# Loading the caches and large weights from GpSimd's DMA queue, one packet per engine and transfer

## The chip, the cores and the metric

The kernel runs on one core of a Trainium2 chip. Its engines are TensorE (PE, whose weight loads the profile shows as PEld), VectorE (DVE), ScalarE (ACT), GpSimd (POOL) and SyncE (SP), and sixteen DMA engines move data between the chip's main memory (HBM) and the on-chip memory (SBUF). The metric is the device time of one execution in microseconds; lower is better. Before the change three runs gave 2522.07, 2522.24 and 2522.47 us, a median of 2522.24.

## The reference, cut to what matters

One decode step of an attention block with a cache of 65,536 positions and 32 heads, and beside it a small gated feed-forward block; a sigmoid gate mixes the two. All inputs are bfloat16.

```python
q = (x @ wq).reshape(1, 1, 32, 128).transpose(0, 2, 1, 3)         # x: 1x1x512, wq: 512x4096
scores = einsum("bhqd,bhkd->bhqk", q, k_cache) * 128 ** -0.5      # k_cache: 1x32x65536x128
p = softmax(scores, axis=-1)
o = einsum("bhqk,bhkd->bhqd", p, v_cache)                         # v_cache: 1x32x65536x128
a = o.transpose(0, 2, 1, 3).reshape(1, 1, 4096) @ wo              # wo: 4096x512
b = (silu(x @ w_gate) * (x @ w_up)) @ w_down                      # 512x1792, 512x1792, 1792x512
g = sigmoid((x * gate_w).sum(-1, keepdims=True))
out = g * a + (1 - g) * b
```

The two caches are 512 MiB each. Every byte of them is used once, so the kernel reads 1,088 MB and computes little on each byte.

## The kernel before, in words

Each head's cache of 65,536 positions is laid over the 128 partitions, 512 positions to a partition, so that a partition's share is one contiguous run of 128 KB. A head is cut into three pieces of 168, 168 and 176 positions per partition (`CUTS`), which makes 96 pieces of K and 96 of V. A piece of 168 is 128 runs of 43,008 bytes, 5.5 MB; a piece of 176 is 128 runs of 45,056 bytes.

SBUF holds a ring of four slots (`SLOTS`), each as large as the largest piece. `big` takes the slot that has been free longest; `load` (L139 to L148) takes a slot and issues the transfer of one piece at L147, in one transfer or, for a few pieces, in several. The query weights `wq` and the feed-forward weights pass through the same ring at the start, and the output weights at the end.

The main loop runs over the K pieces n = 0 to 95. At stage n it issues the load of K piece n and then that of a V piece v that lies up to five pieces behind. It then computes:

- `products` (L304, L308), on DVE: K times the query, in place, and then three halving additions, which leave 16 columns for each position.
- `scores` (L325), on PE: matmuls with the identity add these columns up three at a time into PSUM; this is the last use of the K piece and frees its slot. `add_up` (L343) on DVE finishes the sum one stage later.
- at a head's end `row_max` and `exponentials`: maximum over the head, then the exponentials on ACT.
- `values` (L401), on PE: one matmul for each four positions, against the V piece; the last one frees V's slot.

A load is issued as soon as the last reader of its slot's old content is done. That reader is PE, in `scores` for a slot that held K and in `values` for one that held V. All issues but one stand in SyncE's queue, in program order, and each waits at its head of the queue for its slot and for its completion counter to be free. The one other, `x_row`, is issued by ACT.

SyncE also issues 40 small loads of output-weight rows (`load_tall`, L208) at five places of the main loop, which the matmuls of `project_tall` use nine stages later. After the loop the last V pieces are loaded in up to five transfers each, and `load_wo` (L237) issues the rest of the output weights in ten transfers: five of 512 KB, three of 256 KB and two of 128 KB. The end is the projection (L513), a copy on ACT and the store of the result (L637).

GpSimd does nothing but set constants and build the identity (`make_identity`, behind L97) in the first 1.3 us. The order of all instructions on each engine is the program's (`manual_schedule`).

Of the kernel before, what the change touches and what calls it, by code (L numbers as in the profile page):

```python
# [35 lines left out]
def kernel(  # L36
# [14 lines left out]
    nc = tc.nc  # L51
# [6 lines left out]
    KT = D // P  # L58
    FT = F // P
# [25 lines left out]
    def big(name):  # L85
        slot = free.pop(0)
        t = ring.tile([P, SLOT * Dh], bf16, name=name, tag=f"big{slot}")
        return t, slot
# [4 lines left out]
    gw_row = small.tile([1, D], bf16, name="o_row")  # L93
    wq_t, wq_slot = big("wq_t")
    wq_sb = wq_t[:, : KT * H * Dh].rearrange("p (t f) -> p t f", t=KT)
    nc.sync.dma_start(out=wq_sb, in_=A_wq.rearrange("(p t) f -> p t f", t=KT))
    nc.scalar.dma_start(out=x_row, in_=A_x[0])  # L97

    ident_f = consts.tile([P, P], f32, name="ident_f")
# [36 lines left out]
    def span(n):  # L136
        return CUTS[n % G], CUTS[n % G + 1]

    def load(dst, cache, n, name, cuts=None):  # L139
        h = n // G  # L140
        a, b = span(n)
        t, taken[name, n] = big(name)
        view = t[:, : (b - a) * Dh].rearrange("p (j d) -> p j d", d=Dh)
        src = cache[0, h, :, :].rearrange("(p j) d -> p j d", p=P)
        cuts = cuts or (0, b - a)
        for c, d in zip(cuts[:-1], cuts[1:]):
            nc.sync.dma_start(out=view[:, c:d, :], in_=src[:, a + c : a + d, :])  # L147
        dst[n] = view  # L148

    load(K_tiles, A_k_cache, 0, "K_t", (0, span(0)[1] // 2, span(0)[1]))  # L150
    load(K_tiles, A_k_cache, 1, "K_t")

    def queries(g):
# [17 lines left out]

    gu_t, gu_slot = big("gu_t")
    wgu_sb = gu_t[:, : 2 * KT * F].rearrange("p (w t f) -> p w t f", w=2, t=KT)
    nc.sync.dma_start(out=wgu_sb[:, 0], in_=B_w_gate.rearrange("(p t) f -> p t f", t=KT))
    nc.sync.dma_start(out=wgu_sb[:, 1], in_=B_w_up.rearrange("(p t) f -> p t f", t=KT))
    wd_sb = gu_t[:, 2 * KT * F : 2 * KT * F + FT * D].rearrange("p (t n) -> p t n", t=FT)
    nc.sync.dma_start(out=wd_sb, in_=B_w_down.rearrange("(p t) n -> p t n", t=FT))
    nc.sync.dma_start(out=gw_row, in_=gate_w.rearrange("(o d) -> o d", o=1))
    WG = 4
    wo_tiles = {}  # L180
# [46 lines left out]
    def load_wo():  # L227
        t = big("wo_t")[0]
        for g in range(1, H // WG):
            at = (g - 1) * WG * D  # L230
            wo_tiles[g] = t[:, at : at + WG * D].rearrange("p (t n) -> p t n", t=WG)
            rows = A_wo[g * WG * P : (g + 1) * WG * P, :]
            last = g == H // WG - 1
            rows = rows.rearrange("(t p) n -> p t n" if last else "(p t) n -> p t n", t=WG)
            cuts = (0, 2, 3, 4) if last else (0, 2, 4) if g == H // WG - 2 else (0, 4)
            for a, b in zip(cuts[:-1], cuts[1:]):
                nc.sync.dma_start(out=wo_tiles[g][:, a:b, :], in_=rows[:, a:b, :])  # L237

    def feed_forward_in():

# [298 lines left out]
    rows = {}  # L539
# [15 lines left out]
    for n, v in steps:  # L555
        if n > 1:
            load(K_tiles, A_k_cache, n, "K_t")
# [64 lines left out]
    head_column(H - 2, O_parts)  # L622
    load(V_tiles, A_v_cache, N - 1, "V_t", V_CUTS[N - 1])
    load_wo()
    values(N - 3, 88)
    values(N - 2)
# [41 lines left out]
```

## Time and profile before

| what | value |
|---|---|
| median of three runs | 2522.24 us (2522.07 to 2522.47) |
| span of the profiled execution, first to last instruction | 2520.4 us (the profile gives no other time of it) |
| DMA traffic | 1,088.41 MB in 31,101 packets, 432 GB/s over the span |
| SyncE's DMA queue (q1) | 31,046 packets, 99.9% of sixteen engines' span |
| DVE busy | 2234.4 us, 89% |
| PE busy | 1408.6 us, 56% |
| ACT busy | 103.4 us, 4% |
| GpSimd (POOL) busy | 0.7 us |
| PE waiting for V loads, in total | 774.9 us |
| DVE waiting for K loads, in total | 163.1 us |

The profile is of one execution. Its page gives busy times for each engine, the span in 40 slices with the DMA engines' busy share and rate, the packets of each DMA queue, and the chain of work that ended last, followed back from the last instruction. Besides the page the trace can be asked for windows of time, for the chain in order of time, for what each engine waited for, and for single instructions. It holds a record of every DMA packet with its queue, start, length and bytes. An engine's name with a small q (SPq) is its queue of DMA issues.

### The profile page before, as it was taken

How to read it: one execution, taken by the hardware profiler on the slowest of the kernel's cores; microseconds unless marked ns; L12 is line 12 of the kernel's file. 1: busy time of each engine (PE TensorE's matmuls, PEld its weight loads, DVE VectorE, ACT ScalarE, POOL GpSimd, SP SyncE). 2: the span in 40 equal slices, each digit the busy share in tenths (PEclk: the TensorE clock that was granted, in tenths of full speed). 3: DMA queues.
4: the chain of work that ended last, by engine and by line, in shares of the span. 5: the costliest groups of instructions: out<-in, count | busy, mean ns of one | idle time of the engine just before them, and what ended most of it. 6: DMA issues, size and time to landing. Idle time of an engine off the chain costs nothing.

```text
span 2520.4 us, 12122 instructions
## 1 busy us (share of the span) xinstructions
PE 1408.6 (56%) x5174; PEld 488.2 (19%) x5174; DVE 2234.4 (89%) x788; ACT 103.4 (4%) x314; POOL 0.7 (0%) x6
## 2 busy tenths in 40 slices
PE   2555546565555654655546565554564655556468
PEld 1111112121121211211212121111121211112123
DVE  7999998988989889999889998889999889898880
ACT  1000000000000000000000000000000000000000
POOL 0000000000000000000000000000000000000000
PEclk7677767676776766677767777776677777777779
DMA  9999999999999999999999999999999999999999
GB/s 420 430 439 433 433 431 435 431 433 434 434 432 436 433 434 433 432 434 433 431 434 435 435 433 431 434 433 433 433 433 433 436 434 434 433 432 431 434 434 390
DMA packets 31101, 1088.41 MB, mean 432 GB/s; under 512 B 3532, under 2 KB 4048, under 8 KB 5192
## 3 DMA queue, kind: packets, MB, share of 16 engines
q1 hardware_dynamic: 31046, 1087.65, 99.9%
q8 instruction: 40, 0.66, 0.1%
q14 instruction: 13, 0.11, 0.0%
q10 hardware_dynamic: 2, 0.00, 0.0%
HBM read 1087.64 MB, written 0.00 MB: 432 GB/s over the span
## 4 chain that ended last, share of the span: by engine, by line
DMA 59%; DVE 23%; PE 17%; issue 1%; ACT 0%; SPq 0%; DVEq 0%
DMA V_t<-in_A_v_cache_dram 45%; DMA K_t<-in_A_k_cache_dram 14%; PE O_ps L401 13%; DVE K_t L304 11%; DVE K_t L308 10%; PE part_ps L325 3%; DVE S_sb L343 0%; PE mT_ps L363 0%; DVE m L358 0%; DMA wo_t<-in_A_wo_dram 0%; ACT diag L360 0%; DVE top L370 0%; DVE rg L391 0%; PE a_ps L291 0%; DVE recip L390 0%
## 5 line engine op out<-in xcount | busy, mean ns | idle before, releaser
L401 PE MATMUL O_ps<-V_t,P_sb 128*4 128x512 bf16 x4096 | 1087.3, 434 | 777.8 <-DMA V_t<-in_A_v_cache_dram 774.9
L304 DVE TENSOR_TENSOR K_t<-K_t,q_bc 128x22528 bf16<-128x22528 bf16 (+4 forms) x128 | 1111.9, 8686 | 163.5 <-DMA K_t<-in_A_k_cache_dram 163.1
L308 DVE TENSOR_TENSOR K_t<-K_t 128x5376 bf16<-128x5376 bf16 (+11 forms) x384 | 1016.3, 2647 | 12.2
L401 PEld LDWEIGHTS <-P_sb 128*4 128x4 bf16 x4096 | 383.5, 94 | 1492.8 <-issue 1082.7
L325 PE MATMUL part_ps<-K_t,ident_b 128*128 128x504 bf16 (+2 forms) x640 | 228.8, 506 | 167.9 <-DVE K_t L308 167.9
L325 PEld LDWEIGHTS <-ident_b 128*128 128x128 bf16 x640 | 62.5, 109 | 310.8 <-issue 211.5
L363 PE MATMUL mT_ps<-diag,ones_f 128*128 128x129 f32 (+1 forms) x64 | 24.9, 491 | 130.3 <-ACT diag L360 130.3
L432 ACT ACTIVATE O_sb<-O_ps,ident_f 4x128 f32<-4x128 f32 x120 | 33.2, 346 | 1002.9 <-PE O_ps L401 1002.9
L343 DVE TENSOR_REDUCE S_sb<-part_ps 128x168 f32<-128x504 f32 (+1 forms) x96 | 59.8, 623 | 3.2 <-PE part_ps L325 3.2
L370 DVE TENSOR_REDUCE top<-mT_ps 128x1 f32<-128x128 f32 x32 | 9.3, 292 | 44.8 <-PE mT_ps L363 44.8
L363 PEld LDWEIGHTS mT_ps<-diag,ones_f 128*128 128x128 f32 x64 | 15.6, 303 | 154.6 <-ACT diag L360 154.2
L461 ACT ACTIVATE o_row<-r_sb,rg 1x128 bf16<-1x128 f32 x26 | 10.4, 401 | 581.3 <-DVE r_sb L444 581.3
L439 PE MATMUL r_ps<-O_sb,ones_f 4*1 4x512 f32 x60 | 33.0, 630 | 0.0
L360 ACT ACTIVATE diag<-ident_f,m 128x128 f32<-128x128 f32 x32 | 12.8, 401 | 428.1 <-DVE m L358 428.1
L374 ACT ACTIVATE P_sb<-S_sb,bias 128x512 bf16<-128x512 f32 x32 | 23.1, 722 | 1.0
L358 DVE TENSOR_REDUCE m<-S_sb 128x1 f32<-128x512 f32 x32 | 22.0, 686 | 1.1
L444 DVE TENSOR_REDUCE r_sb<-r_ps 1x128 f32<-1x512 f32 x30 | 20.1, 670 | 0.0
L156 PE MATMUL qg_ps<-wq_t,X_bc 128*128 128x512 bf16 x32 | 9.2, 460 | 10.7 <-DMA wq_t<-in_A_wq_dram 10.7
L390 DVE RECIPROCAL recip<-tot_ps 128x1 f32<-128x1 f32 x1 | 0.2, 168 | 16.6 <-PE tot_ps L385 16.6
L291 PE MATMUL a_ps<-O_sb,ones_f 1*1 1x512 f32 x2 | 1.9, 1030 | 19.7 <-ACT O_sb L290 19.7
L372 ACT ACTIVATE bias<-top 128x1 f32<-128x1 f32 x32 | 6.5, 203 | 41.2 <-DVE top L370 41.2
L246 PEld LDWEIGHTS <-gu_t 128*128 128x128 bf16 x112 | 6.9, 157 | 0.6 <-issue 0.6
(68 smaller groups left out, 88.5 us busy)
## 6 DMA issues: line engine op xcount, KB each, us to landing
K_t<-in_A_k_cache_dram SPq DMA_DIRECT2D x63, 5376.0 KB
V_t<-in_A_v_cache_dram SPq DMA_DIRECT2D x62, 5376.0 KB
K_t<-in_A_k_cache_dram SPq DMA_DIRECT2D x32, 5632.0 KB
V_t<-in_A_v_cache_dram SPq DMA_DIRECT2D x31, 5632.0 KB
V_t<-in_A_v_cache_dram SPq DMA_DIRECT2D x2, 2816.0 KB
K_t<-in_A_k_cache_dram SPq DMA_DIRECT2D x2, 2688.0 KB
V_t<-in_A_v_cache_dram SPq DMA_DIRECT2D x2, 2560.0 KB
wq_t<-in_A_wq_dram SPq DMA_DIRECT2D x1, 4096.0 KB
```

Of the source, the lines that this page charges most:

```text
L304: yield nc.vector.tensor_tensor(out=K, in0=K, in1=q_rep, op=ALU.mult)
L308: yield nc.vector.tensor_tensor(out=K[:, :, 0:half], in0=K[:, :, 0:half], in1=K[:, :, half : 2 * half], op=ALU.add,)
L325: nc.tensor.matmul(part[:, :, 0:take], lhsT=ident_b, rhs=K_tiles[n][:, :, c : c + take], start=(i == 0), stop=(i == len(takes) - 1),)
L343: nc.vector.tensor_reduce(out=S_tiles[h][:, a:b], in_=S_parts.pop(n), axis=AXIS.X, op=ALU.add)
L358: nc.vector.tensor_reduce(out=m, in_=S_tiles[h], axis=AXIS.X, op=ALU.max)
L360: nc.scalar.activation(out=diag[:, :P], in_=ident_f, func=ACT.Copy, scale=m)
L363: nc.tensor.matmul(mT_ps[:, :wide], lhsT=ones_f, rhs=diag[:, :wide], start=True, stop=True)
L374: nc.scalar.activation(out=P_tiles[h], in_=S_tiles[h], func=ACT.Exp, bias=bias, scale=scale, accum_out=new_sum(h),)
L401: nc.tensor.matmul(O_tiles[h], lhsT=P_tiles[h][:, a + j : a + j + 4], rhs=V_tiles[n][:, j : j + 4, :], start=(a + j == 0), stop=(a + j == ...
L432: nc.scalar.activation(out=O_sb[:, c * Dh : (c + 1) * Dh], in_=O_ps[:, c * Dh : (c + 1) * Dh], func=ACT.Copy, scale=ident_f[0:4, c : c + 1],)
L439: nc.tensor.matmul(r_ps, lhsT=ones_f[0:4, 0:1], rhs=O_sb, start=True, stop=True)
L444: nc.vector.tensor_reduce(out=r_sb, in_=r_ps.rearrange("o (c d) -> o d c", c=4), axis=AXIS.X, op=ALU.add)
```

## The change

[...] For a K or V piece an engine's part is eight runs, one for each of eight partitions. Sizes, order and destinations stay. `x_row` stays on ACT; `gate_w`, the 40 small output-weight loads and the store of the result stay on SyncE.

```diff
-    nc.sync.dma_start(out=wq_sb, in_=A_wq.rearrange("(p t) f -> p t f", t=KT))
+    nc.gpsimd.dma_start(single_packet=True, out=wq_sb, in_=A_wq.rearrange("(p t) f -> p t f", t=KT))
...
         for c, d in zip(cuts[:-1], cuts[1:]):
-            nc.sync.dma_start(out=view[:, c:d, :], in_=src[:, a + c : a + d, :])
+            nc.gpsimd.dma_start(
+                out=view[:, c:d, :], in_=src[:, a + c : a + d, :], single_packet=True
+            )
...
-    nc.sync.dma_start(out=wgu_sb[:, 0], in_=B_w_gate.rearrange("(p t) f -> p t f", t=KT))
-    nc.sync.dma_start(out=wgu_sb[:, 1], in_=B_w_up.rearrange("(p t) f -> p t f", t=KT))
+    nc.gpsimd.dma_start(single_packet=True, out=wgu_sb[:, 0], in_=B_w_gate.rearrange("(p t) f -> p t f", t=KT))
+    nc.gpsimd.dma_start(single_packet=True, out=wgu_sb[:, 1], in_=B_w_up.rearrange("(p t) f -> p t f", t=KT))
...
-    nc.sync.dma_start(out=wd_sb, in_=B_w_down.rearrange("(p t) n -> p t n", t=FT))
+    nc.gpsimd.dma_start(single_packet=True, out=wd_sb, in_=B_w_down.rearrange("(p t) n -> p t n", t=FT))
...
-                nc.sync.dma_start(out=wo_tiles[g][:, a:b, :], in_=rows[:, a:b, :])
+                nc.gpsimd.dma_start(
+                    out=wo_tiles[g][:, a:b, :], in_=rows[:, a:b, :], single_packet=True
+                )
```

## The prediction

> **What bounds the kernel.** I read the page from the top: busy times, the 40 slices, the DMA queues, the chain that ended last, the costly groups.
>
> ```profile
> span 2520.4 us, 12122 instructions
> ...
> PE 1408.6 (56%) x5174; PEld 488.2 (19%) x5174; DVE 2234.4 (89%) x788; ACT 103.4 (4%) x314; POOL 0.7 (0%) x6
> ...
> DMA  9999999999999999999999999999999999999999
> GB/s 420 430 439 433 433 431 435 431 433 434 434 432 436 433 434 433 432 434 433 431 434 435 435 433 431 434 433 433 433 433 433 436 434 434 433 432 431 434 434 390
> DMA packets 31101, 1088.41 MB, mean 432 GB/s; under 512 B 3532, under 2 KB 4048, under 8 KB 5192
> ...
> q1 hardware_dynamic: 31046, 1087.65, 99.9%
> q8 instruction: 40, 0.66, 0.1%
> ...
> DMA V_t<-in_A_v_cache_dram 45%; DMA K_t<-in_A_k_cache_dram 14%; PE O_ps L401 13%; DVE K_t L304 11%; DVE K_t L308 10%; PE part_ps L325 3%; DVE S_sb L343 0%; PE mT_ps L363 0%; DVE m L358 0%; DMA wo_t<-in_A_wo_dram 0%; ACT diag L360 0%; DVE top L370 0%; DVE rg L391 0%; PE a_ps L291 0%; DVE recip L390 0%
> ...
> L304 DVE TENSOR_TENSOR K_t<-K_t,q_bc 128x22528 bf16<-128x22528 bf16 (+4 forms) x128 | 1111.9, 8686 | 163.5 <-DMA K_t<-in_A_k_cache_dram 163.1
> L308 DVE TENSOR_TENSOR K_t<-K_t 128x5376 bf16<-128x5376 bf16 (+11 forms) x384 | 1016.3, 2647 | 12.2
> ```
>
> The sixteen DMA engines are busy in every slice, at 430 to 436 GB/s nearly everywhere; queue q1, which is SyncE's, has 99.9% of it. DVE at 89% is the next bound, some 286 us away. PE and DVE wait, in the chain, for K and V loads. So the end is set by how long the DMA engines take over 1,088 MB, plus a start before their first packet and a tail behind their last.
>
> Two things about that DMA time decide this case: what a packet costs besides its bytes, and how early a load is issued. For the first, the windows view (second column of numbers from the right is the DMA share, the last is GB/s):
>
> ```profile
> 2016.00:2457.00 441.00, 243.91 (x872) 82.77 (x872) 396.36 (x133) 16.30 (x51) 0.00 (x0) 0.73 1.00 433
> 2490.00:2500.00 10.00, 9.56 (x45) 3.68 (x44) 0.00 (x0) 0.00 (x0) 0.00 (x0) 1.00 1.00 423
> 2500.00:2505.00 5.00, 4.26 (x20) 1.61 (x19) 0.00 (x0) 0.00 (x0) 0.00 (x0) 1.00 1.00 424
> 2505.00:2510.00 5.00, 5.00 (x24) 1.94 (x23) 0.00 (x0) 0.00 (x0) 0.00 (x0) 1.00 0.97 394
> ```
>
> At a full DMA share the rate is 433 GB/s where the packets are 43,008 and 45,056 bytes, but 423 where the last V pieces and the output weights move 5 to 20 KB at a time: small packets are dearer per byte. The trace's packet records give the size of it: 43,008 bytes take 1.589 us (median of 16,000), 4,096 bytes 0.159 us (median of 648), the 4 bytes of a completion 0.009 us. The slope is 38,912 B / 1.430 us = 27.2 B/ns for one engine, and what is left over is 1.589 - 43,008 / 27,200 = 0.008 us, at 4,096 bytes also 0.008. Each packet costs 8 ns beside its bytes, whatever its size.
>
> For the second, the chain between two heads (start, length, what):
>
> ```profile
> 235.30 36.07 DMA V_t<-in_A_v_cache_dram
> 271.37 0.04 issue
> 271.41 11.93 PE O_ps L401 x42
> 283.34 0.02 issue
> 283.36 27.32 DMA K_t<-in_A_k_cache_dram
> ```
>
> A V load lands 36 us after SyncE issued it, a K load 27.3 us after. Its own 5.5 MB take 12.7 us at 433 GB/s, so a K load stood behind 27.3 - 12.7 = 14.6 us of other transfers, less about 2 us of start and receipt (from the output's issue at 2518.46 us to the end of the span at 2520.4 is 1.9): a lead of some 12.6 us. V has some 21 us. The smallest lead, at the start, is about 5 us (V issued at 94.96, landed 19.8 us later). In steady state a K issue may come 12 us late and the engines still don't run dry.
>
> **The change part by part.**
>
> *Packets.* The moved loads are 97 K and 102 V issues, one wq, three feed-forward weights and ten output weights: 213. They hold 199 x 128 (caches) + 128 (wq) + 384 (feed-forward) + 1,408 (output weights: 5 x 128, 2 x 128, 4 x 128 rows) = 27,392 data packets, 1,712 per engine, and 213 completions per engine. With all of one engine's rows of a load in one packet, up to 1,712 of its 1,925 gaps can go: 1,712 x 8.2 ns = 14.0 us, all on the path, since the DMA engines are never idle. That is the best end. The middle end is nothing, if the 8 ns belong to each contiguous run and not to the packet; the worst end is a loss, if a packet of 344 KB (8 x 43,008) starts less smoothly than one of 43 KB (third rival). The trace can't separate run and packet, since here each run is a packet. The nearest row is the 4-byte completion: 9 ns for a packet with almost no bytes, so the gap goes with the packet's opening and closing. I take most of it, 10 us, and leave 4 us for what each run inside a packet may still cost.
>
> [...]
>
> *The issue moves from SyncE to GpSimd.* SyncE's issue instruction lasts 0.33 us (median of 199 at the load's line). GpSimd has 0.7 us of work in the whole span, all before 1.3 us, so 213 issues find a free queue; what one costs there the trace does not show. Two loads fall due per 25.5 us; between 0.33 us and 5 us an issue lies within the lead of 12.6 us and costs nothing. If that cover were gone, each us past it would cost 97 us, one for each K.
>
> *Start.* wq's issue on SyncE begins at 0.74 us, its first packet some 1.0 us later. GpSimd is past the opening barrier at 0.73, too, so the shift is only the difference in issue latency: between 0 and 3 us (nine times SyncE's issue). I take 0.6, nearer to the rows of SyncE and ScalarE (0.41 and 0.51 us for their first issues). It delays the DMA stream, so it counts in full. The identity that GpSimd builds behind wq's issue is needed at 41.9 us, by the first scores: hidden.
>
> *Tail.* The ten output-weight loads go one by one between 2482.6 and 2511.2 us, held back by earlier landings; the last lands at 2516.95. With a slower issue the DMA share of that stretch, 0.83 to 0.97 already, can lose 0 to 1.5 us. I take 0.5.
>
> *What leaves SyncE's queue.* The 40 small output-weight loads stay on SyncE and no longer stand before a K load (at 211.74 four of them took 9.74 us, waits included). That only lengthens a lead: nothing. An engine that changes queues only between packets would now keep such a load waiting up to 12.7 us in place of 1.6; they are used nine stages (230 us) later: nothing. The instruction fetches (q8, 40 packets of 16 KB; by their number PE's, which has 10,348 of the 12,122 instructions) could wait as long. PE waits 775 us in all for V loads, so a stall of 11 us mostly falls into that; at most 40 x 11 us, taken into the range's upper part.
>
> *Sum.* 2520.4 - 10 + 0.6 + 0.5 = 2511.5 us of span. The three timed runs have a median of 2522.24, 1.8 us above the profiled span (the profiled execution is known by its span alone), so 2513.3: I say 2513. Its own range, with 14.0 or 6 us saved and the small terms at their ends, is 2508 to 2518.
>
> **The rivals.**
>
> *The gap belongs to each run, nothing is saved.* For it: each partition's row is a contiguous run of its own before and after. Against it: the 9 ns of a 4-byte packet. Only start and tail are left: 2523.3, range 2518 to 2528, which is no change.
>
> *DVE holds up GpSimd's issues, and the engines run dry (slower).* Place: K's issue, which always comes just ahead of DVE's longest instruction:
>
> ```profile
> 283.36 0.33 SPq L147 DMA_DIRECT2D K_t<-in_A_k_cache_dram  x1
> ...
> 284.65 11.89 DVE L304 TENSOR_TENSOR K_t<-K_t,q_bc 128x22528 bf16<-128x22528 bf16 x1 [3.11 <-DMA K_t<-in_A_k_cache_dram]
> ```
>
> The K load is issued 1.3 us before L304 starts 11.9 us of work. If GpSimd could not write its descriptors until that instruction ends, the issue would be 13.2 us late, plus 1 us of its own: 14.2 against a lead of 12.6. It decides from there: 1.6 us x 97 = 155 us, 2677. If it needed the next instruction's end also (L308, 5.4 us), 7 us x 97 = 680 us, 3200. If only some issues were caught, 2540 to 2600. For it: DVE is busy 89% of the span. Against it: what these two engines share cannot be seen here, as GpSimd does nothing after 1.3 us.
>
> [...]
>
> *A long packet starts cold (slower).* The first sixteen packets of the run, 32,768 bytes on idle engines, took 1.8 to 2.2 us against 1.21 later: filling the pipe costs 0.6 to 1.0 us. If every load's packet paid that, 213 x 0.75 = 160 us: 2682; a tenth of it gives 2539. For it: nothing shows how descriptors reach the engines from GpSimd. Against it: a load is issued 12 us ahead, which is time to fetch them.
>
> **How the numbers follow.** Three runs of before lie within 0.4 us, so 0.2%, 5 us, is about what can be told from no change. Saved packets 0.50; nothing saved 0.19; issues held up 0.16; cold packets 0.15. The first gives faster, the second the same, the other two slower: 0.50, 0.19, 0.31. The first two fill 2507 to 2528 with 0.69; of the slower 0.31 about 0.11 are mild forms up to 2570, so 2507 to 2570 holds 0.80.
>
> **What would show it.** Right: q1 nearly empty, a queue of GpSimd with 1,087 MB, 434 to 435 GB/s in the steady slices, a DMA share of 1.00, and 43,008 bytes at 1.581 to 1.585 us in the packet records. Nothing saved: 1.589 again and 433 GB/s. Held up: slices with DMA below 9, POOL's queue waiting or its issues lasting as long as L304. Cold: long first packets of each load, and the rate down evenly. The prediction is wrong if the steady rate is below 432 GB/s, or if the landing of a K load is more than 30 us behind its slot's release.

## The result and the profile after

The changed kernel takes 2525.74 us (median of 20 runs, 2525.19 to 2527.21), the kernel before 2522.32 (20 runs, 2522.07 to 2522.49): a ratio of 1.0014, with a 95% interval of 1.0008 to 1.002. It is slower by 3.4 us, 0.14%, clear of the noise and within the 0.2% that the prediction calls no change. The forecast was 2513 us.

The page of the changed kernel (columns as on the page of before; in section 6 the last column is the median time from issue to landing):

```profile
span 2524.4 us, 12148 instructions
...
PE 1412.3 (56%) x5174; PEld 488.7 (19%) x5174; DVE 2234.4 (89%) x788; ACT 103.5 (4%) x314; POOL 113.6 (4%) x219
...
DMA  9999999999999999999999999999999999999998
GB/s 415 432 430 433 434 433 436 432 433 433 433 433 435 432 433 434 436 433 432 432 434 433 435 435 430 433 435 433 434 433 434 431 434 433 433 436 431 433 432 370
DMA packets 30589, 1088.41 MB, mean 431 GB/s; under 512 B 3532, under 2 KB 3536, under 8 KB 4680
...
q0 software_dynamic: 30288, 1087.12, 99.7%
q8 instruction: 40, 0.66, 0.1%
q1 hardware_dynamic: 246, 0.53, 0.1%
...
L147 POOL DMA_DIRECT2D K_t<-in_A_k_cache_dram x97 | 51.3, 529 | 1918.5 <-PE O_ps L405 1523.2
...
K_t<-in_A_k_cache_dram POOLq DMA_DIRECT2D x63, 5376.0 KB, 27.1
V_t<-in_A_v_cache_dram POOLq DMA_DIRECT2D x62, 5376.0 KB, 36.8
```

The traffic has moved to GpSimd's queue (q0), all else is as it was: 430 to 436 GB/s in the steady slices, the DMA engines at 9 tenths or more in all slices but the last. There are 512 packets fewer, not 27,000. An issue costs GpSimd 0.53 us where SyncE needed 0.33, and a K load still lands 27 us after it. In the windows view (last columns granted clock, DMA share, GB/s) the stages that hold 95% of the time have the rates of before to 1 GB/s. The first line is of before, whose second stage the prediction shows, the other two are of after:

```profile
63.00:2016.00 1953.00, 1088.99 (x3856) 368.87 (x3855) 1790.14 (x625) 76.70 (x240) 0.00 (x0) 0.73 1.00 433
...
63.00:2016.00 1953.00, 1089.22 (x3848) 368.54 (x3848) 1790.53 (x626) 76.61 (x239) 79.79 (x151) 0.72 1.00 433
2016.00:2457.00 441.00, 245.06 (x875) 82.88 (x874) 397.53 (x133) 16.50 (x52) 18.11 (x35) 0.74 1.00 434
```

The packet records say the same: 43,008 bytes take 1.589 us (median of 16,000), as before. With each packet's bytes spread evenly over its record, 1,000 MB of the loads have moved 2310.53 us after the first packet, before 2310.47. So in this execution the way between the two ends costs and gains nothing. The profiled execution (2526.15 us itself, its span 2524.4) differs from before's at the ends:

| stretch of the profiled span | before | after | difference |
|---|---|---|---|
| start of the span to the first data packet | 1.77 | 2.62 | +0.85 |
| first data packet to the last | 2515.53 | 2516.20 | +0.67 |
| last data packet to the store's issue | 1.16 | 1.22 | +0.05 |
| store's issue to the end | 1.96 | 4.33 | +2.37 |

The store's issue, before and after:

```profile
2518.46 0.28 SPq L637 DMA_DIRECT2D out_dram<-out_sb  x1
...
2520.04 0.26 SPq L641 DMA_DIRECT2D out_dram<-out_sb  x1
```

The last row of the table is the largest. Beside the kernel's work, the program ends with a meeting: its closing line has drains and semaphore instructions of all five engines. In the changed kernel GpSimd comes to it last, when the other four have drained by 2521.6 us. Its drains, in the source view of the program's closing line (shortest, median and longest in ns, then first and last start), of before and of after:

```profile
L663 POOLq DRAIN  x3: 34/77/386, 1.0 to 2520.2; - x3
```

```profile
L667 POOLq DRAIN  x3: 45/102/10457, 2513.1 to 2524.1; - x3
```

The long one starts at 2513.1 us, with GpSimd's last load issued, and lasts 10.46 us, to 2523.6. That is 4.8 us after the last data packet (2518.82) and 2.0 after SyncE was ready. SyncE's waits in the closing (the sum, how often, the longest; the view names the last engine by its semaphore, not GpSimd) show what it costs, before and after:

```profile
SPq L663 <- PEq L663: 0.6, 2, 0.4
```

```profile
SPq L667 <- PEq L667: 2.7, 2, 2.2
```

### The profile page after: what moved, and what is told of

The parts are those of the page before. It is cut to its first block, busy times and chain, and to the rows that moved or that the text cites. A ratio compares the mean times of both kernels' runs of the same rounds, so it can differ in the third digit from the quotient of the medians.

```text
span 2524.4 us, 12148 instructions
## 1 busy us (share of the span) xinstructions
PE 1412.3 (56%) x5174; PEld 488.7 (19%) x5174; DVE 2234.4 (89%) x788; ACT 103.5 (4%) x314; POOL 113.6 (4%) x219
## 4 chain that ended last, share of the span: by engine, by line
DMA 66%; DVE 18%; PE 13%; issue 3%; ACT 0%; POOL 0%; DVEq 0%; POOLq 0%
DMA V_t<-in_A_v_cache_dram 60%; PE O_ps L405 10%; DVE K_t L308 9%; DVE K_t L312 8%; DMA K_t<-in_A_k_cache_dram 4%; PE part_ps L329 2%; DMA wo_t<-in_A_wo_dram 1%; DMA wq_t<-in_A_wq_dram 1%; DVE S_sb L347 0%; PE qg_ps L158 0%; PE mT_ps L367 0%; DVE m L362 0%; PE a_ps L517 0%; ACT diag L364 0%; PE a_ps L295 0%
## 5 line engine op out<-in xcount | busy, mean ns | idle before, releaser
L147 POOL DMA_DIRECT2D K_t<-in_A_k_cache_dram x97 | 51.3, 529 | 1918.5 <-PE O_ps L405 1523.2
L147 POOL DMA_DIRECT2D V_t<-in_A_v_cache_dram x102 | 53.9, 528 | 451.4 <-PE part_ps L329 344.1
## 6 DMA issues: line engine op xcount, KB each, us to landing
K_t<-in_A_k_cache_dram POOLq DMA_DIRECT2D x63, 5376.0 KB, 27.1
```

The source lines that it names most:

```text
L147: nc.gpsimd.dma_start(out=view[:, c:d, :], in_=src[:, a + c : a + d, :], single_packet=True)
```

## The experiments

Beside each experiment the kernel before was timed on the same chip; its medians are 2522.28 to 2522.39 us. Differences to the changed kernel go by its 2525.74. Line numbers of the experiments differ by a few.

**The option off, and the option on SyncE's queue.** Two changes were made at once, a queue and an option (`single_packet=True`); these take them apart.

```diff
-nc.gpsimd.dma_start(..., single_packet=True)
+nc.gpsimd.dma_start(...)                        # e1_no_option
...
-nc.gpsimd.dma_start(..., single_packet=True)
+nc.sync.dma_start(..., single_packet=True)      # e2_option_on_sp
```

> The changed kernel with the one-packet option taken off every load; the queue stays GpSimd's. Theory (an 8 ns gap belongs to each long run of bytes, the option saves nothing on runs of 43 KB, and the loss lies at the start, in the tail and in the closing): as the changed kernel, 2525.7 us within 0.5, with 43,008 bytes at 1.589 us again. Rival A (the option saves some of the gap and the queue loses more elsewhere): slower than the changed kernel, up to 2539. Rival B (the long packets are what costs): nearer to the kernel before, 2522.3 to 2524.

> The changed kernel with every load issued by SyncE again, the one-packet option left on. Theory: the kernel before, 2522.3 us, packets and all, as the option would have nothing to act on there. Rival A (the option works on either queue): 2508 to 2517.

Measured: 2525.55 us without the option (11 runs, 2525.30 to 2527.08), 2522.37 with it on SyncE's queue (10 runs, 2522.18 to 2522.54), against 2522.38 for the kernel before. The theory held in both. The queue line of the first is the changed kernel's, packet for packet:

```profile
q0 software_dynamic: 30288, 1087.12, 99.7%
```

So the option does nothing here on either queue, and the whole 3.4 us belong to the queue. One packet for all that an engine moves of a transfer, as the title has it, is found in no run; whether the option reached the queues at all, the traces do not tell. The joining of the last output weights' 1 and 2 KB rows, which is where the 512 packets went, is done by GpSimd's queue without it.

**What a run costs.** The cache rows are cut into four runs, on each queue, and then into runs of 2 KB.

```diff
-    nc.sync.dma_start(out=view[:, c:d, :], in_=src[...])
+    nc.sync.dma_start(out=view[:, c:d, :], in_=src[...], max_dma_last_dim=11264)    # e3; 2048 in e5
...
-    nc.gpsimd.dma_start(..., single_packet=True)
+    nc.gpsimd.dma_start(..., single_packet=True, max_dma_last_dim=11264)            # e4; 2048 in e6
```

> The kernel before, with each partition's run of a cache piece cut into four (10,752 or 11,264 bytes). 4,512 runs more per engine for the 188 full pieces and 48 for the cut ones, 4,560 x 8.2 ns = 37.4 us. Every theory: 2559.7 us. It gives the price of a run on SyncE's queue.

> [...] Theory (the gap belongs to the run): 2525.7 + 37.4 = 2563.1 us, packet records of 10,752 bytes at 0.40 us. Rival A (the gap belongs to the packet, and the option makes one packet of all): 2525.7 us.

Measured: 2543.74 us on SyncE's queue, 2544.89 on GpSimd's (four runs each). Both expectations of size missed: on SyncE's queue 4,560 more runs cost 21.4 us, 4.7 ns each, where the packet records leave 8 ns over. On GpSimd's they cost 2544.89 - 2525.74 = 19.2 us, 4.2 ns each, so what one packet would have saved (all of it) is not saved. And the two queues are now 1.15 us apart, not 3.4, of which more below.

> The kernel before with cache rows cut into runs of 2,048 bytes: 31,180 runs more for each engine. By 4.7 ns a run (21.4 us / 4,560 in the quarter cut): 2669 us. By the packet records' 8.2 ns: 2778 us. This is the price for the next.

> The changed kernel with the same runs of 2,048 bytes (168 and more for one engine and transfer). Theory (GpSimd's queue joins runs into packets of 4,096 bytes and no more, as it did with the 1 and 2 KB rows of the last output weights): packet records of 4,096 bytes at 0.159 us and half the added price, 2595 to 2605 us. Rival (nothing is joined): 2,048-byte records and 2657 to 2672 us. Rival (all in one packet): 2526 us.

Measured: 2669.36 and 2612.82 us (two runs each). The first confirms the price. By the pages there are 500,224 packets more than before, 31,264 for each engine where the expectation had 31,180, so a run costs 147.0 us / 31,264 = 4.70 ns. The pages, first on SyncE's queue, then on GpSimd's:

```profile
GB/s 400 409 409 409 409 409 409 409 409 409 409 409 409 409 409 407 409 409 409 408 409 409 410 409 409 409 409 409 409 409 409 409 409 409 409 409 409 409 409 378
DMA packets 531325, 1088.41 MB, mean 408 GB/s; under 512 B 3532, under 2 KB 10448, under 8 KB 530760
...
q1 hardware_dynamic: 531270, 1087.65, 104.6%
```

```profile
GB/s 400 418 418 418 418 418 418 418 418 418 418 418 418 418 418 418 418 418 418 418 419 418 418 418 418 419 418 418 418 418 418 418 418 418 418 418 418 418 418 379
DMA packets 266877, 1088.41 MB, mean 417 GB/s; under 512 B 3532, under 2 KB 3568, under 8 KB 266312
...
q0 software_dynamic: 266576, 1087.12, 101.8%
...
L147 POOL DMA_DIRECT2D K_t<-in_A_k_cache_dram x97 | 133.8, 1380 | 1952.4 <-PE O_ps L406 1574.4
```

GpSimd's queue joins two runs into a packet of 4,096 bytes (260,544 records of that size, none of 2,048): 267 thousand packets in place of 531. The pieces with shorter runs show where it stops: three runs of 1,408, 1,536 or 1,792 bytes make packets of 4,224, 4,608 and 5,376 bytes, four of 1,280 make 5,120. So it joins runs until a packet holds 4,096 bytes or more; the 4,096 bytes "and no more" of the expectation are the case of 2 KB runs.

That costs 87.1 us more than the changed kernel, somewhat over the 70 to 80 expected. Per engine there are 14,768 packets more than in the changed kernel; at 4.70 ns they come to 69.4 us, and the other 17.7 us, over 16,496 joined runs, are 1.1 ns each. If the closing is taken out, which is 2.0 us shorter here than in the changed kernel, they are 1.2 ns. A packet saved is therefore worth 3.5 to 3.6 ns, less than half of the 8 ns that the forecast took from the records. This takes the 4.7 ns of SyncE's queue for GpSimd's too; with the same 2.0 us of closing taken out, the quartered runs cost 4.6 ns there. Runs of 4 KB and more were joined in no run here, with the option or without.

The queue's share on the page of the first, 104.6% of sixteen engines, also says why the records mislead: the records of one engine overlap. A record's length holds time in which the engine already works on the next.

**The ends, by moving loads.** Four kernels give single loads at the ends back to SyncE or, in the last, one load to GpSimd. The lines are shortened; in the first three GpSimd's loads keep the option.

```diff
-    nc.gpsimd.dma_start(single_packet=True, out=wq_sb, ...)                  # e7, and e9
+    nc.sync.dma_start(out=wq_sb, ...)
...
-                nc.gpsimd.dma_start(out=wo_tiles[g][:, a:b, :], ...)         # e8, and e9
+                (nc.gpsimd if g < H // WG - 2 else nc.sync).dma_start(out=wo_tiles[g][:, a:b, :], ...)
...
-                nc.sync.dma_start(out=wo_tiles[g][:, a:b, :], ...)           # e11, from the kernel before
+                (nc.gpsimd if last and b == 4 else nc.sync).dma_start(out=wo_tiles[g][:, a:b, :], ...)
```

> The changed kernel with wq alone issued by SyncE again. The first packet should come 0.85 us earlier (1.77 us as in the kernel before, not 2.62). Theory (start, tail and closing add up, about 0.85 + 0.67 + 2.4 of the profiled span): 2525.7 - 0.85 = 2524.9 us. Rival (the first packet's delay is made up later, since GpSimd's other issues follow it anyway): 2525.7 us.

> The changed kernel with the last five output-weight loads (1 MB) issued by SyncE again; GpSimd's last issue then is some 10 us earlier. Theory (GpSimd's drain ends about 10 us after its last issue begins, and the closing waits for it): the drain ends before the store, the closing falls from 4.3 us after the store's issue to about 2.3, and the tail gets back part of its 0.67: 2523.1 to 2523.8 us. Rival (the closing takes 2 us more whenever GpSimd has issued loads, early or late): 2525.0 to 2525.7.

> Both: wq and the last five output-weight loads by SyncE, the caches and all else by GpSimd. Theory: the two gains add, 2522.3 to 2523.0 us, so the caches alone cost or gain nothing on GpSimd's queue. Rival (the queue costs something in steady state, too): over 2523.5.

> The kernel before, with only the very last output-weight load (128 KB) issued by GpSimd, every other load by SyncE. Theory (drain after GpSimd's last issue): the closing takes 2 us longer with this one load, 2524.3 to 2524.8 us, with a drain of about 10 us in GpSimd's queue. Rival (the closing grows with the 213 loads): 2522.3 to 2522.8.

Measured: 2525.27 (2524.52 to 2526.40), 2525.73, 2525.74 and 2522.72 us, eleven runs each. Only the first is near its theory: 0.47 us less than the changed kernel where 0.85 was expected, in runs that spread over 1.9 us. The other three tested less than I meant, for the same reason. With two queues the order of the program no longer set the order of landing here. SyncE has nothing else to wait for, so it issues the five late loads of the second kernel at 2480.7 us, ahead of output weights that GpSimd issues up to 2504.7. They push back V's last pieces, and from the last packet to the store there are 3.5 us of work left in place of 1.2. The closing did fall in the second kernel, from 4.33 to 2.02 us after the store's issue, but the store came 1.9 us later. The time of the last kernel lies in its rival's range, but there GpSimd issued its only load at 2479.7, not last, so its drain (7.1 us, to 2486.8) was over long before the end, and the 0.4 us say nothing on the closing. The order is lost at the start, too. In the first kernel SyncE issues wq at 0.74 us as before, but GpSimd's first K loads share the engines with it, and the query matmuls start at 17.8 us (in the changed kernel at 14.1):

```profile
0.74 0.41 SPq L96 DMA_DIRECT2D wq_t<-in_A_wq_dram  x1
...
17.83 8.97 PE L158 MATMUL qg_ps<-wq_t,X_bc 128*128 128x512 bf16 x32 [15.52 <-DMA wq_t<-in_A_wq_dram]
```

**The ends, with the last V piece as well.** This was to keep the tail's order by giving SyncE all of it.

```diff
-            nc.gpsimd.dma_start(out=view[:, c:d, :], ..., single_packet=True)
+            if name == "K_t" or n < N - 1: nc.gpsimd.dma_start(..., single_packet=True)
+            else: nc.sync.dma_start(...)        # and wq and all of load_wo on nc.sync
```

> wq, the last V piece and all output weights by SyncE, in the order and with the holding back of the kernel before; all other loads by GpSimd with the option. Theory (all of the loss lies at the two ends): first packet at 1.77 us, GpSimd's drain over before the store, 2522.3 to 2522.8 us. Rival (GpSimd's queue costs something on the way): 2523.5 or more.

Measured: 2534.93 us (five runs), 12.5 over before. The theory's figure failed, and the rival's holds for a reason that is not the rival's. The chain at its end (start, length, what):

```profile
2460.53 48.61 DMA V_t<-in_A_v_cache_dram
2509.13 0.04 issue
2509.18 15.49 PE O_ps L406 x64
2524.67 0.87 PE a_ps L518 x8
2525.55 0.98 PE oc_ps L426 x8
2526.52 5.35 PE a_ps L518 x48
```

The last DMA packet ends at 2519.6 us, 2.3 later than in before, after an equal start. But the V piece that GpSimd issued at 2460.5 took 48.6 us to land, as SyncE's later loads (issued from 2469.4 us) shared the engines with it, and when it was there all of the last matmuls were still to be done. The DMA engines finished almost as early, in the wrong order.

**The closing.** How long after the last landing of GpSimd's loads its drain ends: 0.41 us with 1 load (e11), 4.76 with 213 (the changed kernel), 2.11 with 213 loads of four times the runs (e4), 1.22 with those of 2 KB (e6). That is why the two queues are 1.15 us apart with quartered runs: there the drain is over before the store is, and the closing takes 2.31 us. The author's theory for it, which no trace shows, was that the drain works through finished loads that GpSimd still keeps on lists, and that lists filled by longer loads are cleared sooner. Two experiments: fewer loads, and `dynamic_dma_scratch_size=4096`, which was meant to make the lists smaller.

```diff
-            nc.gpsimd.dma_start(out=view[:, c:d, :], ..., single_packet=True)         # e12
+            if n >= 66: nc.gpsimd.dma_start(..., single_packet=True)
+            else: nc.sync.dma_start(...)        # wq and feed-forward weights on nc.sync
...
-    nc = _bacc.Bacc("TRN2", target_bir_lowering=False, num_devices=1)                 # e14, e15
+    nc = _bacc.Bacc("TRN2", target_bir_lowering=False, num_devices=1, dynamic_dma_scratch_size=4096)
```

> wq, the feed-forward weights and the caches' first two thirds by SyncE; from piece 66 on, and for the output weights, GpSimd: 76 loads in place of 213. GpSimd's closing drain ended 4.76 us after its last landing with 213 loads, 4.71 with 212, 4.49 with 208, 4.45 with 207: 0.052 us per load, and 2.11 with 213 loads of four times as many runs. Theory D (the drain retires the loads that GpSimd has not yet retired, about 85 of 213, and none is retired earlier while there are few): 76 loads cost about 4.3 us after the last landing, the closing is as long as in the changed kernel, 2524.4 to 2525.3 us. Rival (the drain grows with all loads in the run, 4.76 / 213 = 0.022 us each): 1.7 us, which the store covers, 2522.5 to 2523.2 us.

> [...] The quarter-run kernels differed by 1.15 us between the two queues, not 3.4, and there the drain ended 2.11 us after the last landing, not 4.76. Theory (the closing drain works through the finished loads still on the lists; here at most some 28 of them, by 41 ns each 1.5 us, which the store covers): closing 2.3 us after the store's issue, not 4.3, and 2523.4 to 2524.0 us. Rival (the drain depends on the number of loads alone): 2525.3 to 2526 us.

> The same with wq issued by SyncE. Theory (start and closing are all of the loss): first packet at 1.77 us, 0.85 us less than the small ring alone, 2522.6 to 2523.1 us. Rival (the queue costs something on the way): 2523.5 or more.

Measured: 2524.92, 2523.59 and 2523.42 us. With 76 loads the drain ended 3.47 us after the last landing, between the theory's 4.3 and its rival's 1.7, but the closing is only 3.05 us, and the total is mixed with a loss of 2.1 us at the change of queues (the stream falls that far behind the kernel before's between 730 and 760 MB moved), so its falling into the theory's range proves little. It does exclude that every load of the run adds the same: 76 loads cost 73% of what 213 did.

With the scratch size set, the drain costs less: same loads, same order, same queue, and 2.15 us less. What the drain works through is not shown, and no run shows the 28 loads or the 41 ns for each that the expectation adds up; its range held. GpSimd's drain and SyncE's wait:

```profile
L669 POOLq DRAIN  x3: 40/102/7074, 2512.8 to 2521.8; - x3
```

```profile
SPq L669 <- PEq L669: 0.7, 2, 0.5
```

The drain ends 1.36 us after the last landing, inside the time that the store takes anyway, and the closing is 2.33 us. With wq on SyncE besides, the first packet came at 1.76 us as expected, but only 0.17 us were gained; the expectation missed.

## Why the prediction was wrong, point by point

- *Packets*, the step that failed. The forecast took 10 us for packets that would vanish. No run shows that, nor the 6 us saved at the small end of its range. None of the cache's packets vanished: the option changed no packet in any run here, and GpSimd's queue joined only runs under 4 KB. The rival "the gap belongs to each run, nothing is saved", with 2523.3 us and a range of 2518 to 2528, was the right case, with a chance of 0.19; its 2523.3 lacked the closing. The signs that the prediction named for being wrong did not appear (433 GB/s, over its 432; K loads landing in 27.1 us, under its 30). The sign that told was the 1.589 us of a record, for nothing saved.
- *The size of the gap* was wrong as well. A packet's 8 ns in the records is no time lost, since records overlap (104.6% of the engines' span in e5); a run cost 4.7 ns when the number of runs was changed. All 1,712 gaps could have given 8.0 us, not 14.0, and at 3.5 to 3.6 ns for a joined packet 6.0 to 6.2.
- *The nearest row*, the 9 ns of a 4-byte completion, was no argument. Such a completion is a packet and a run, and could not tell one from the other, as the prediction itself had said of the rest.
- *The issue* at no cost was right. It takes 0.53 us in place of 0.33, under a lead of 12.6; K loads land in 27.1 us, before 27.3 for the one shown. At 2 KB runs it takes 1.38 us, and the slices stay level at 418 GB/s.
- *DVE holds up GpSimd's issues* did not happen. The stretch that the prediction showed, in the timeline of after:

```profile
283.51 0.53 POOL L147 DMA_DIRECT2D K_t<-in_A_k_cache_dram  x1 [20.90 <-PE O_ps L405]
...
285.58 11.89 DVE L308 TENSOR_TENSOR K_t<-K_t,q_bc 128x22528 bf16<-128x22528 bf16 x1 [3.19 <-DMA K_t<-in_A_k_cache_dram]
...
285.60 0.53 POOL L147 DMA_DIRECT2D V_t<-in_A_v_cache_dram  x1 [1.56 <-PE part_ps L329]
```

  A V load is issued 0.02 us after DVE starts its longest instruction, and takes 0.53 us. All 199 issues of the caches took 0.528 to 0.552 us (source view of L147), with DVE busy for 89% of the span. The rival's chance of 0.16 was the author's estimate.
- *A long packet starts cold* was not tested: there is no long packet.
- *Start*: 0.6 forecast, 0.85 measured in the profile. GpSimd starts its first issue at 1.25 us, not at 0.73 where its first work behind the opening barrier had started before, and needs 0.67 us for it. Two lines of before, then after:

```profile
0.73 0.20 POOL masks.py:197 MEMSET ident_f<- 128x128 f32 x1 [0.29 <-POOLq L652]
0.74 0.41 SPq L96 DMA_DIRECT2D wq_t<-in_A_wq_dram  x1
...
1.25 0.67 POOL L96 DMA_DIRECT2D wq_t<-in_A_wq_dram  x1 [0.80 <-POOLq L656]
1.91 0.22 POOL masks.py:197 MEMSET ident_f<- 128x128 f32 x1
2.21 0.29 POOL masks.py:199 TENSOR_SCALAR_AFFINE_SELECT ident_f<-ident_f 128x128 f32<-128x128 f32 x1
2.45 1.60 POOL L147 DMA_DIRECT2D K_t<-in_A_k_cache_dram  x3
```

- *Tail*: 0.5 forecast; 0.67 in this profile, but 0.05 in the one without the option and 0.38 in e14, so it is of the size of the spread between executions.
- *Missing*: the closing. The sum had no term for what GpSimd does at the end of the program, which costs 2.4 us of the profiled span. Some 2.0 are the drain, and most of the rest are SyncE's semaphore instructions ahead of its own drain, nine in 1.14 us where there had been five in 0.83.
- *Two slips in the working* changed nothing in the outcome. The range's upper end does not follow from its terms: 6 us saved, with 3 of start and 1.5 of tail, is 2520.7 us, not 2518. And the last load landed at 2517.30 us by the packet records; 2516.95 is the landing of another, in the chain.

The 3.4 us are thus 2.1 for the drain (e14, in timed runs) and 1.3 for the rest, in which the profile has 0.85 for the start and 0.37 for the closing without the drain (2.33 us in e14, 1.96 before). The profile without the option, of an execution at its kernel's median, has the same parts with almost no tail: 0.86 of start, 0.05 of tail, 0.05 before the store and 2.37 of closing.

What stays open is the start in timed runs. In the profiled executions the earlier first packet is kept: at 1,000 MB moved, counted from the start of the span, the stream is 0.91 us behind the kernel before's in the changed kernel and 0.07 with wq on SyncE, 1.17 in e14 and 0.17 in e15. So the late query matmuls did not slow the stream. But the gain in timed runs was 0.47 and 0.17 us. Where loads came from GpSimd and a kernel was timed eleven times or more, its runs, but for the one with a single such load, also spread over 1.1 to 2.2 us from run to run, before over 0.5.

One place where the profiled executions part can be named. It is the short lead at the start that the prediction put at about 5 us. The K load behind it, before and after:

```profile
110.11 0.33 SPq L147 DMA_DIRECT2D K_t<-in_A_k_cache_dram  x1
...
112.31 0.53 POOL L147 DMA_DIRECT2D K_t<-in_A_k_cache_dram  x1 [14.88 <-PE O_ps L405]
```

In the kernels with whole runs that leave this load to GpSimd it is issued at 111.2 to 112.9 us, and between 40 and 100 MB moved (95 to 234 us) their streams fall behind the kernel before's by another 0 to 0.7 us: 0.08 in the changed kernel, nothing without the option, 0.32 in e14, 0.71 in e13. With this load on SyncE it is at most 0.04. How much of the spread in timed runs comes from there, nothing here tells. No version was faster than the kernel before.

## What to carry to other kernels

Here a queue was changed for next to nothing on the way (433 GB/s before and after) and still cost at both ends (0.85 and 2.37 us in the profiled executions): add up when the first packet leaves, and what the issuing engine has to finish before the program can close. Before a saving per packet is booked, change the number of packets and time it; a packet record's length was not time lost where the records added up to more than the engines' time (104.6% in e5). Loads on two queues did not land in the order of the program here, and moving a few of them to save a microsecond cost 12.5 us over the kernel before (e13).

## What the runs showed of the hardware that was not expected

- A run that is a packet costs 4.7 ns of an engine's time (21.4 us for 4,560 in e3, 147.0 us for 31,264 in e5), and 1.1 to 1.2 ns when it is joined to others (e6, worked out with the 4.70 ns). A packet's record shows 8 to 9 ns over its bytes when it is one run, and 9 to 14 as a median when two to four runs are joined in it (e6).
- GpSimd's queue joined runs of 1 to 2 KB until a packet held 4,096 bytes or more (packets of 4,096 to 5,376 bytes in e6), those of the last output weights with or without the one-packet option; runs of 4,096 bytes and more stayed single.
- GpSimd's long drain at the end ended 0.41 (e11) to 4.76 us (the changed kernel) after the last landing of GpSimd's loads. `dynamic_dma_scratch_size=4096` took this from 4.76 to 1.36 us, and the kernel from 2525.74 to 2523.59 us (e14). That it is finished loads which the drain works through is the author's theory; the traces do not show it.
- GpSimd's issue takes 0.53 us at 128 runs, 0.74 at 512 and 1.38 at 2,688 and more, 0.3 to 0.6 ns for each run added.
